# Strassen's form for three pairs of chunks instead of two, x from whole float32 operands, and a planner that counts the port of VectorE and GpSimd

## The chip, the cores and the metric

The kernel runs on one core of a Trainium2 chip. The core has TensorE (PE, matrix products into PSUM), VectorE (DVE), ScalarE (ACT), GpSimd (POOL) and SyncE (SP, which here only issues DMAs). Each engine works through its own list of instructions in order and waits at semaphores. The metric is device time in microseconds (us), lower is better.

## What is computed

```python
kv  = einsum('bhsd,bhse->bhde', k, v)      # 8 batches, 8 heads, s = 576, d = e = 64
o   = einsum('bhsd,bhde->bhse', q, kv)
x   = o / sqrt(mean(o*o, -1) + 1e-6) * g_norm       # per head
x   = x.transpose(0, 2, 1, 3).reshape(4608, 512)    # 4608 tokens, 8 heads x 64
h   = x @ w_in                                      # 512 x 2048
out = (h * cos(h)) @ w_out                          # 2048 x 512
```

All inputs and the output are float32.

## The kernel before

**Tiling.** The 4608 tokens are nine chunks of 512 (`CH`), numbered 0 to 8; the 2048 columns of `h` are 16 blocks `j` of 128 (`NJ`). `NP = 4` is the number of head pairs: the 512 columns of x are four blocks `p` of 128, each of two heads. `x_part(c, p)` makes one such block of one chunk, transposed (128 features by 512 tokens); a chunk covers parts of one or two batches (`chunk_parts`).

**Precision.** The big products are done in a float32 format that TensorE streams at one pass (`F32R`, "fp32r" in the profile). Each operand is split into a high part and a rest (`xhi`, `xlo`; `ghi`, `glo`; two halves of each weight tile), and three products replace one.

**Stage 1 and stage 2, plain.** Step `(c, j)` of `stage1_part` makes block j of h for chunk c: 4 p x 3 products of 512 columns. `act_part` turns it into g = h cos h on ACT and DVE and splits it (`ghi`, `glo`); `stage2_part` multiplies with `w_out`: 4 accumulators (`acc`) x 3 products. Chunks 0 and 1 go first and are interleaved in four segments while the weights are still loaded and split (`w_part`).

**Stage 1 by Strassen's form.** Two chunks and two halves of the 512 features form a 2x2 block product. Seven products of combined operands replace eight. `cross_part` makes the seven combinations of x (adds and splits on POOL or DVE: `adders()` lets the planner choose); `sums_part` makes combined weights on POOL from the split ones, and `keep_in`, `keep_out`, `sums_part` write all weights to DRAM (`wq`, `wod`), since their places in SBUF are then used for the crosses, for x (`raws`) and for g. `quad_part(n)` does the seven products of two blocks j (7 x 6 matmuls) and adds them up through `snap` and `add`; `chain_part` makes g, `split_part` and `gather_part` do stage 2. `load_in` and `load_out` bring the weights back from DRAM for each pair.

Before the change `PLAIN = 5`: chunks 0 to 4 are plain (`NS` = 80 steps), chunks 5, 6 and 7, 8 are two pairs (16 quads).

**x.** For chunks 2 to 8, `kv_part(b)` makes the 64x64 products k'v of one batch in float32: per head pair and head four matmuls of 128 rows and one for the last 64 rows (`k_over`, `v_over`, whose rows 64 to 127 are zero). `kv_parts` writes them to `kv_w` in split form. `x_part` loads q (`q_loads`, eight to sixteen small DMAs), transposes it on DVE (`qT`), splits it for the two heads on ACT and DVE or POOL into tiles `m` and `sg`, multiplies with `kv_w` into two PSUM banks, adds their halves on ACT and DVE, then makes the norm: square (ACT), transpose and sum (DVE), a power -0.5 on POOL (`rinv`), transpose and scaling with `gcol` (DVE). Chunks 0 and 1 use routines of their own (`kv_front_part`, `x_front_part`).

**What sets the order.** The class `Order` is a planner that runs while the program is built: every routine is a generator that asks for time on an engine with a duration, a priority, events and tokens for buffers; the planner always takes the piece that can start first, and that is then the order on the engine (`Pinned`). Priorities come from due times (`due(i)` for step i) plus a table of offsets, `haste`. `gates[i]` fires when step i starts on PE, and routines are let in by it. In the profile every operation has line 206, the helper that records it; operations are told apart by tiles: `bank` are PSUM banks of h, kv, x and transposes, `acc` the accumulators, `wi`/`wo` places of weight tiles, lent to k, v, q at the start and to crosses, g and reloaded weights later.

Of the kernel before, what the change touches and what calls it, by code (L numbers as in the profile page):

```python
# [49 lines left out]
class Order:  # L50
# [11 lines left out]
    def __init__(self):  # L62
        self.busy = {}
        self.pending = []
        self.seq = 0
        self.live = set()
        self.shape = None
# [51 lines left out]
    def ahead(self, e, prio, options):  # L119

        if len(options) == 1:
            return 0.0
        now = self.busy.get(e, 0.0) + 0.2
        return sum(o[0][1] for x, _, t, o, _ in self.pending if len(o) == 1 and o[0][0] == e and x <= prio and t <= now)

    def run(self):
        while self.pending:
            best = None
            for item in self.pending:
                prio, seq, t, options, _ = item  # L130
                ends = [
                    max(t, self.busy.get(o[0], 0.0) + self.ahead(o[0], prio, options)) + o[1] + sum(o[2:])
                    for o in options
                ]
                e, d = options[ends.index(min(ends))][:2]
                start = max(t, self.busy.get(e, 0.0))
                if best is None or (start, prio, seq) < best[0]:
                    best = ((start, prio, seq), item, e, d)
# [8 lines left out]
            end = start + d  # L147
            self.busy[e] = end
# [5 lines left out]
def tile_kernel(  # L154
# [22 lines left out]
    ST = S - SI * P  # L177

# [47 lines left out]
    def dve_only(f):  # L226
        return [("DVE", 0.15 + f / 960)]

    def adders(f=CH, late=0.4):

        return [("POOL", 0.2 + f / 460, 0.0), ("DVE", dve_us(f), late)]
# [7 lines left out]
    kv_w = const.tile([P, 2, H, P], F32R, name="kv_w")  # L239
    warm = const.tile([P, 1], F32, name="warm")  # L240
# [21 lines left out]
    PLAIN = 5  # L262
# [16 lines left out]
    KEEP, SUMS = 34, 40  # L279

    def due(i):
# [7 lines left out]
        ('load q', 0, 1): -62.5, ('acc', 32): 88.0, ('acc', 20): -37.8, ('xd', 7, 3): -3.4, ('unit', 4): 2.6,  # L289
        ('unit', 1): 46.8, ('h', 27): -11.0, ('h', 72): 24.3, ('load q', 1, 1): -3.5, ('cross', 1, 0): 10.5,  # L290
        ('h', 35): 35.9, ('act', 17): 80.9, ('h', 21): -12.0, ('unit', 6): 21.5, ('x', 1, 3): -3.5,
        ('quad', 2): -16.7, ('acc', 21): 19.0, ('load', 'wo', 1): -22.6, ('act', 73): 32.8, ('act', 7): 28.5,
        ('xd', 5, 3): 49.3, ('xd', 6, 1): -11.9, ('acc', 58): 83.2, ('unit', 42): 95.7, ('unit', 11): 45.8,
# [3 lines left out]
        ('h', 70): -15.1, ('act', 0): -23.3, ('load kv', 0, 2): 17.8, ('load', 'wi', 3): 42.2, ('acc', 4): 76.7,  # L297
        ('load kv', 0, 0): 18.4, ('wo', 2): -38.8, ('h', 3): -33.0, ('xd', 8, 0): 70.4, ('load q', 0, 3): 5.7,
        ('h', 58): -11.0, ('acc', 19): -35.6, ('h', 61): -46.5, ('acc', 0): 51.2, ('act', 75): 10.5,
        ('x', 0, 2): 4.0, ('load kv', 0, 3): -7.5, ('h', 75): 26.1, ('acc', 57): 27.1, ('h', 19): 18.3,  # L300
        ('xd', 3, 1): -23.0, ('wo', 12): -1.4, ('h', 12): 8.9, ('xd', 5, 1): -8.5, ('acc', 61): 48.1,
        ('unit', 2): -14.5, ('act', 53): 40.4, ('acc', 9): 10.8, ('h', 68): -6.9, ('acc', 28): 14.4,
        ('h', 42): -9.5, ('h', 65): -5.5, ('act', 65): -18.0, ('h', 60): -4.3, ('wo', 8): 7.8,
        ('split', 13): -14.3, ('quad', 0): -2.5, ('wi', 15): 16.8, ('acc', 18): 12.2, ('xd', 2, 2): -19.3,
    }

    def put_off(*key):
        return haste.get(key, 0.0)

# [57 lines left out]
    def g_part():  # L367
        yield "wait", [g_in]
        yield "run", [("ACT", 0.4)], -11.0
# [14 lines left out]
    def over_loads(b):  # L384
        def issue():
            for t, src in ((k_over, k), (v_over, v)):
                nc.sync.dma_start(out=t[0:ST], in_=src[b, :, SI * P:S, :].rearrange("h p d -> p h d"))
# [116 lines left out]
    def kv_parts(b, srcs, prio):  # L504

        for j, src in enumerate(srcs):
# [9 lines left out]
    def kv_part(b, prio):  # L516
# [36 lines left out]
    def x_front_part(c, p, prio):  # L553
# [53 lines left out]
        yield "run", [("POOL", 1.4)], prio  # L607
# [20 lines left out]
        _, end = yield "run", dve_only(CH), prio  # L628
# [9 lines left out]
    def x_part(c, p, prio):  # L638
# [3 lines left out]
        yield "take", t_two, prio  # L642
# [5 lines left out]
        rows = [slice(j * D, (j + 1) * D) for j in range(2)]  # L648
        qs = [two([P, CH], F32R, j) for j in range(2)]
# [21 lines left out]
        if c < PLAIN:  # L671
            x_slot = yield "take", t_slot, prio
            x = slot_tile(x_slot)
        else:
            held = yield "take", t_raw, prio
            x = store_tile(held)
# [7 lines left out]
        sched.give(t_pair, end)  # L684
# [710 lines left out]
```

## Time and profile before

| | us |
|---|---|
| median of 3 runs | 854.68 (854.52 to 856.24) |
| profiled execution, its own time | 853.01 |
| its span, first to last instruction | 851.2 |
| PE busy / DVE busy / ACT busy / POOL busy | 830.2 / 614.3 / 512.0 / 233.2 |
| chunk 5's first quad starts on PE at about | 500 |

Matmuls are pipelined: the records of 512 columns last 390 ns each and overlap, so a count over a stretch, and not the mean, tells what one costs. A float32 matmul has two records. In a row of a timeline stand the start, the time, the engine, line, operation, tiles, shape and count; in a row by stretches the busy time and the number of instructions of PE, weight loads, DVE, ACT and POOL, then the granted clock, DMA share and GB/s.

### The profile page before, as it was taken

What the parts mean: (1) busy time and instruction counts of PE and PEld (TensorE: products, weight loads), DVE (VectorE), ACT (ScalarE), POOL (GpSimd) and SP (SyncE); (2) the same over time, 40 slices, a digit from 0 to 9 for tenths busy, and PEclk for the clock granted to TensorE, in tenths of its full rate; (3) what the DMA queues carried; (4) which work ended last, traced back from release to release, by engine and by line L of the source; (5) the groups of instructions that cost most, each with busy time, mean ns of one, the idle gap of its engine ahead of it and who ended that gap; (6) DMA issues with size and microseconds to landing.
All of it is one profiled execution on the core that took longest, in us unless ns stands there. A gap on an engine that the chain in (4) does not pass through costs nothing.

```text
span 851.2 us, 12582 instructions
## 1 busy us (share of the span) xinstructions
PE 830.2 (98%) x4400; PEld 686.0 (81%) x4400; DVE 614.3 (72%) x947; ACT 512.0 (60%) x993; POOL 233.2 (27%) x151
## 2 busy tenths in 40 slices
PE   6899999999999999999999999999999999999998
PEld 5778888888888888788888887888788788888886
DVE  2899897489697647868688998899898754445421
ACT  3789685476465547545577657767676554444421
POOL 3220000014135564647313453522444100000000
PEclk9899999999999999999999999999999999999999
DMA  9989746163421324521624357767656566754564
GB/s 304 326 279 380 293 185 223 47 168 96 124 50 51 112 81 129 147 78 54 180 76 113 77 159 219 202 184 217 193 171 237 173 204 194 244 180 143 187 213 144
DMA packets 139968, 145.55 MB, mean 171 GB/s; under 512 B 73216, under 2 KB 112896, under 8 KB 139904
## 3 DMA queue, kind: packets, MB, share of 16 engines
q1 hardware_dynamic: 139392, 144.02, 54.9%
q8 instruction: 35, 0.57, 0.3%
q10 hardware_dynamic: 512, 0.72, 0.2%
q14 instruction: 29, 0.24, 0.1%
HBM read 110.10 MB, written 34.60 MB: 170 GB/s over the span
## 4 chain that ended last, share of the span: by engine, by line
PE 85%; DVE 7%; ACT 2%; issue 2%; POOL 2%; DMA 2%; SPq 1%; ACTq 0%; DVEq 0%; POOLq 0%
PE bank L206 44%; PE acc L206 40%; POOL rinv L206 1%; DVE glo L206 1%; DVE wi L206 1%; DVE wo L206 1%; DVE slot L206 1%; DMA gcol<-in_g_norm_dram 1%; DVE xlo L206 1%; DMA wi<-in_q_dram 1%; DVE qT L206 1%; DVE r L206 1%; ACT wi L206 1%; ACT ki L206 0%; SPq L415 0%
## 5 line engine op out<-in xcount | busy, mean ns | idle before, releaser
L206 PE MATMUL acc<-wo,ghi 128*128 128x512 f32 x1152 | 356.1, 390 | 0.0
L206 PEld LDWEIGHTS acc<-wo,ghi 128*128 128x128 f32 x1152 | 214.8, 188 | 44.1 <-ACT slot L206 0.2
L206 PE MATMUL acc<-wo,glo 128*128 128x512 f32 x576 | 224.5, 390 | 0.0
L206 POOL TENSOR_TENSOR rinv<-ms,mhalf 128x16 f32<-128x16 f32 (+1 forms) x36 | 98.4, 2735 | 306.6 <-DVE ms L206 304.8
L206 PE MATMUL bank<-xhi,wi 128*128 128x512 f32 x576 | 178.3, 391 | 0.0
L206 PE MATMUL bank<-wi,wo 128*128 128x512 f32 (+2 forms) x756 | 165.7, 375 | 4.5 <-DVE wi L206 2.3
L206 PEld LDWEIGHTS bank<-wi,wo 128*128 128x128 f32 (+2 forms) x756 | 128.5, 185 | 34.2 <-DVE wi L206 4.1
L206 PEld LDWEIGHTS acc<-wo,glo 128*128 128x128 f32 x576 | 108.1, 188 | 22.8 <-DVE glo L206 0.2
L206 PEld LDWEIGHTS bank<-xhi,wi 128*128 128x128 f32 x576 | 107.3, 188 | 22.0
L206 PE MATMUL bank<-xlo,wi 128*128 128x512 f32 x288 | 112.2, 390 | 0.0
L206 ACT ACTIVATE ki<-bank 128x512 int32<-128x512 f32 x96 | 57.1, 595 | 55.9 <-PE bank L206 52.8
L206 DVE TENSOR_TENSOR glo<-r,ghi 128x512 fp32r<-128x512 f32 x88 | 66.3, 754 | 23.9 <-ACT ghi L206 22.9
L206 DVE SCALAR_TENSOR_TENSOR r<-bank,ki 128x512 f32<-128x512 f32 x82 | 56.3, 686 | 35.0 <-ACT ki L206 34.0
L206 ACT CAST ghi<-r 128x512 fp32r<-128x512 f32 x89 | 55.2, 620 | 38.9 <-PE acc L206 29.8
L206 ACT ACTIVATE r<-r 128x512 f32<-128x512 f32 x89 | 55.9, 630 | 17.9 <-DVE r L206 17.0
L206 DVE TENSOR_TENSOR r<-r,bank 128x512 f32<-128x512 f32 x82 | 55.7, 681 | 10.9 <-ACT r L206 10.0
L206 PEld LDWEIGHTS bank<-xlo,wi 128*128 128x128 f32 x288 | 54.0, 188 | 11.4
L206 DVE TENSOR_TENSOR glo<-wo,ghi 128x512 fp32r<-128x512 f32 x42 | 31.5, 750 | 36.0 <-ACT ghi L206 34.0
L206 ACT ACTIVATE ki<-wi 128x512 int32<-128x512 f32 x48 | 30.1, 628 | 32.9 <-DVE wi L206 24.9
L206 ACT CAST ghi<-wo 128x512 fp32r<-128x512 f32 x44 | 27.3, 621 | 33.3 <-PE acc L206 31.8
L206 DVE TENSOR_TENSOR wi<-bank,wi 128x512 f32<-128x512 f32 x48 | 32.9, 688 | 11.5 <-PE bank L206 9.4
L206 ACT COPY wi<-bank 128x512 f32<-128x512 f32 x48 | 28.1, 586 | 19.3 <-PE bank L206 18.7
(168 smaller groups left out, 1028.6 us busy)
## 6 DMA issues: line engine op xcount, KB each, us to landing
wo<-wod SPq DMA_DIRECT2D x64, 512.0 KB, 3.4
wo<-wq SPq DMA_DIRECT2D x56, 512.0 KB, 4.2
out_dram<-slot SPq DMA_DIRECT2D x35, 256.0 KB, 2.2
wi<-in_moe_w_in_dram SPq DMA_DIRECT2D x16, 512.0 KB, 8.6
wo<-in_moe_w_out_dram SPq DMA_DIRECT2D x16, 512.0 KB, 8.5
wod<-wo SPq DMA_DIRECT2D x16, 512.0 KB, 5.3
wq<-wi SPq DMA_DIRECT2D x24, 256.0 KB, 4.6
sg<-in_v_dram SPq DMA_DIRECT2D x24, 256.0 KB, 3.9
```

Source lines behind the costliest of these rows:

```text
L206: return lambda *a, **kw: tc.keep_in_program_order(f(*a, **kw))
```

## The change

1. `PLAIN` is 3: chunks 3 and 4 become a third pair, first in time (`NS` = 48 steps, 24 quads). The weights are kept and summed from steps 16 and 18 on instead of 34 and 40, spread over the steps left. A second and third pair's crosses wait for those of the pair ahead.
2. Chunks 2, 3 and 4 (`WHOLE`) get x from `q` and `kv` in whole float32 (`kv_f`): `x_whole` does one matmul per head and part with 64 rows and 64 columns of the array, straight into one bank; the norm (`x_norm`, the old code) reads that bank. The splits and the two banks' additions go.
3. x of chunks 3 and 4 (`ASIDE`) is made in steps 24 to 44, stored to DRAM, and read back when places come free.
4. `k_over`, `v_over` hold a head pair in 128 rows, 64 each, without zeros; their matmuls use 64 rows.
5. The planner: `POOL*` and `DVE*` mark operations with two SBUF operands, and one of them waits for the other (`begin`); durations on POOL are set anew; gates of x and sums can be moved by the table.
6. At the start k and v of the first head pair are issued ahead of all else, and the scaling of `gcol` is planned behind the second pair's loads. The table is new (113 entries for 80).

```diff
     def begin(self, e, t):
+        if e == "POOL*":
+            return max(t, self.busy.get("POOL", 0.0), self.port["DVE"])
+        if e == "DVE*":
+            return max(t, self.busy.get("DVE", 0.0), self.port["POOL"])
+        return max(t, self.busy.get(e, 0.0))
...
-    k_over = const.tile([P, H, D], F32, name="k_over")
-    v_over = const.tile([P, H, D], F32, name="v_over")
-    for t in (k_over, v_over):
-        pool.memset(t[ST:P], 0.0)
+    k_over = const.tile([P, NP, D], F32, name="k_over")
+    v_over = const.tile([P, NP, D], F32, name="v_over")
...
-    PLAIN = 5
+    PLAIN = 3
...
-    KEEP, SUMS = 34, 40
+    KEEP, SUMS = 16, 18
+    WHOLE = (2, 3, 4)
+    ASIDE = (3, 4)
...
     haste = {
-        ('load q', 0, 1): -62.5, ('acc', 32): 88.0, ('acc', 20): -37.8, ('xd', 7, 3): -3.4, ('unit', 4): 2.6,
+        ('kv', 1, 1): 74.8, ('h', 33): 17.7, ('h', 19): 13.3, ('wo', 10): 161.9, ('kv', 0, 3): 15.1,
...
     def g_part():
         yield "wait", [g_in]
+        yield "wait", [kv_in[0, 1]]
...
     def kv_parts(b, srcs, prio):
+        later = [c for c in chunks_of(b) if c >= FRONT]
+        if any(c in WHOLE for c in later):
+            for j, src in enumerate(srcs):
+                _, end = yield "run", [("ACT", act_us(NP * D))], prio
+                act.copy(out=kv_f[j * D:(j + 1) * D, b % 2], in_=src)
+        if all(c in WHOLE for c in later):
+            return end
...
-                        (kt[:, j, i, :], vt[:, j, i, :]) if i < SI else (t[:, 2 * p + j, :] for t in (k_over, v_over)))
+                        (kt[:, j, i, :], vt[:, j, i, :]) if i < SI else (t[r, p, :] for t in (k_over, v_over)))
                     pe.matmul(out=ps[r, p, :], lhsT=lhs, rhs=rhs, start=(i == 0), stop=(i == SI))
...
+    def x_whole(c, p, prio, parts, rows, qT, bank):
+        _, end = yield "run", [("PE", sum(max(0.12, (n + 24) / 600) for _, _, _, n in parts))], -1.0, D
+        ps = ps_tile(bank)[:, 0:CH]
+        for b, s0, o0, n in parts:
+            for r in rows:
+                pe.matmul(
+                    out=ps[r, o0:o0 + n], lhsT=kv_f[r, b % 2, p, :], rhs=qT[r, o0:o0 + n], start=True, stop=True)
+        sched.fire(q_used[c, p], end)
+        sched.give(t_qT, end)
+        x, held = yield from x_place(c, prio)
+        yield from x_norm(c, p, prio, ps, x, held, "DVE", lambda end: give_ps(bank, end))
...
+        if c in ASIDE:
+            _, end = yield "run", [("DMA", 0.9)], prio
+            aside = tc.dram_tile([P, CH], F32, name=f"x{c}_{p}")
+            nc.sync.dma_start(out=aside, in_=x)
+            sched.give(t_slot, end + DMA_LAT, held)
+            stored = Event()
+            sched.fire(stored, end + DMA_LAT)
+            held = yield "take", t_raw, due(begin[PLAIN - 1]) + p
+            yield "wait", [stored]
+            _, end = yield "run", [("DMA", 0.9)], due(begin[PLAIN - 1]) + p
+            x = store_tile(held)
+            nc.sync.dma_start(out=x, in_=aside)
+            end += DMA_LAT
...
-        first, n = (NS + QUAD * NM * (two_chunks - 1), QUAD * NM) if two_chunks else (begin[PLAIN - 1], NJ)
+        first, n = (NS + QUAD * NM * (two_chunks - 1), QUAD * NM) if two_chunks else (begin[PLAIN - 1] - 4, NJ)
...
+        if n:
+            yield "wait", [cross_done[n - 1, q, x] for q in range(7) for x in range(HK)]
...
-            t += put_off("load kv", c, p)
+            t += put_off("load kv", c, p) if c or p else -100.0
...
+            i = min(max(i + step_off("gate x", c, p), last_step[0] + 1 if c < PLAIN else 0), len(gates) - 1)
...
-        sched.spawn(gated(SUMS + 2 * m, sums_part(m, due(SUMS + 3 + 2 * m) + put_off("sums", m))))
+        i = SUMS + m * (NS - SUMS - 6) // NM
+        i = min(max(i + step_off("gate sums", m), 0), len(gates) - 1)
+        sched.spawn(gated(i, sums_part(m, due(i + 3) + put_off("sums", m))))
```

ACT's first instructions before (`wi`/`wo` hold k, v of the first heads, `bank_172` the transposed q):

```order
L206 ACT_TABLE_LOAD
L206 COPY m<-bank_172 128x512
L206 DMA wi_200<-in_k_dram 128x576
L206 DMA wo_201<-in_v_dram 128x576
L206 ACT_TABLE_LOAD
L206 ACTIVATE warm<-warm 128x1
L206 DMA gcol<-in_g_norm_dram 64x1
L206 COPY wo_158<-bank_181 64x64 x2
L206 COPY wo_158<-bank_206 64x64 x2
L206 COPY m<-bank_230 128x512
L206 ACTIVATE gcol<-gcol 64x1 x2
L206 ACTIVATE slot_257<-acc_245 128x512
```

and after:

```order
L222 DMA wi_161<-in_k_dram 128x576
L222 DMA wo_162<-in_v_dram 128x576
L222 ACT_TABLE_LOAD
L222 ACTIVATE warm<-warm 128x1
L222 DMA gcol<-in_g_norm_dram 64x1
L222 COPY wo_157<-bank_173 64x64 x2
L222 COPY m<-bank_198 128x512
L222 ACTIVATE slot_219<-acc_210 128x512
L222 ACTIVATE gcol<-gcol 64x1 x2
```

The loads of k, v and g_norm stand ahead of every computation, one table load is gone, and the first square (`slot`, out of `acc`) stands ahead of the scaling of `gcol`, not behind it.

On PE, the first x part of chunk 2, before:

```order
L206 MATMUL bank_1977<-xlo,wi_1295 128x512
L206 MATMUL bank_1999<-m,kv_w 128x128
L206 MATMUL bank_1999<-m,kv_w 128x384
L206 MATMUL bank_2000<-sg,kv_w 128x128
L206 MATMUL bank_2000<-sg,kv_w 128x384
L206 MATMUL bank_1977<-xhi,wi_1295 128x512 x2
```

and after:

```order
L222 MATMUL acc_1411<-wo_1522,glo 128x512
L222 MATMUL bank_2016<-qT,kv_f 64x128 x2
L222 MATMUL bank_2016<-qT,kv_f 64x384 x2
L222 MATMUL acc_1418<-wo_1522,ghi 128x512 x2
L222 MATMUL acc_1418<-wo_1522,glo 128x512
```

Four matmuls over the whole array into two banks became four over a quarter of it into one, between the same kind of neighbours (stage 1 there, stage 2 here).

On SP, the loads ahead of the first quad's weights, before (chunk 5 is first; `wq` are the weights, `qb` is q of chunks 7 and 8):

```order
L380 DMA m<-in_k_dram 128x2x256
L380 DMA sg<-in_v_dram 128x2x256
L415 DMA qb<-in_q_dram 32x14x32 x4
L415 DMA qb<-in_q_dram 32x2x32 x4
L1064 DMA wo_5254<-wq 128x1024
L415 DMA qb<-in_q_dram 32x14x32 x4
```

and after (chunk 3 is first; `x_3_3475` is the DRAM place of x of chunk 4, pair 3):

```order
L1151 DMA wo_3424<-wq 128x1024
L412 DMA sg<-in_v_dram 128x2x256
L791 DMA x_3_3475<-slot_3292 128x512
L412 DMA sg<-in_v_dram 128x2x256
L799 DMA wo_3044<-x_3_3475 128x512
L1151 DMA wo_3538<-wq 128x1024
L1151 DMA wo_3610<-wq 128x1024
```

A store of x and its reload now stand among the weights' loads, with one other load between them.

More of the change, by code (lines that the diff above doesn't have):

```diff
@@ L63, in __init__ @@
         self.busy = {}
+        self.port = {"POOL": 0.0, "DVE": 0.0}
         self.pending = []
@@ L130, in run @@
                 prio, seq, t, options, _ = item
[L131 to L136, printed above, removed]
+                if len(options) == 1:
+                    e, d = options[0][:2]
+                else:
+                    ends = [
+                        max(t, self.busy.get(o[0].rstrip("*"), 0.0) + self.ahead(o[0].rstrip("*"), prio)) + o[1] + sum(o[2:])
+                        for o in options
+                    ]
+                    e, d = options[ends.index(min(ends))][:2]
+                start = self.begin(e, t)
                 if best is None or (start, prio, seq) < best[0]:
@@ L147, in run @@
             end = start + d
+            if e[-1] == "*":
+                e = e[:-1]
+                self.port[e] = end
             self.busy[e] = end
@@ L226, in dve_only, with pool_us @@
     def dve_only(f):
-        return [("DVE", 0.15 + f / 960)]
+        return [("DVE*", 0.15 + f / 960)]
     def adders(f=CH, late=0.4):
-        return [("POOL", 0.2 + f / 460, 0.0), ("DVE", dve_us(f), late)]
+        return [("POOL*", pool_us(f), 0.0), ("DVE*", dve_us(f), late)]
+    def pool_us(f=CH):
+        return 0.19 + f / 465
     def adder(e):
@@ L239, in tile_kernel @@
     kv_w = const.tile([P, 2, H, P], F32R, name="kv_w")
+    kv_f = const.tile([P, 2, NP, D], F32, name="kv_f")
     warm = const.tile([P, 1], F32, name="warm")
@@ L386, in issue @@
             for t, src in ((k_over, k), (v_over, v)):
-                nc.sync.dma_start(out=t[0:ST], in_=src[b, :, SI * P:S, :].rearrange("h p d -> p h d"))
+                for j in range(2):
+                    nc.sync.dma_start(
+                        out=t[j * ST:(j + 1) * ST],
+                        in_=src[b, :, SI * P:S, :].rearrange("(p two) s d -> two s p d", two=2)[j])
         return issue
@@ L641, in x_part @@
         yield "wait", [q_in[c, p]] + [kv_in[b, n] for b, _, _, _ in parts if b >= FRONT for n in range(NP)]
-        yield "take", t_two, prio
+        if c in WHOLE:
+            yield "wait", [kv_done[b, p] if b >= FRONT else kv_split[b, p] for b, _, _, _ in parts]
+            yield "take", t_psa, prio
+            bank = yield "take", t_bank, prio
+        else:
+            yield "take", t_two, prio
         yield "take", t_qT
@@ L648, in x_part @@
         rows = [slice(j * D, (j + 1) * D) for j in range(2)]
+        if c in WHOLE:
+            yield from x_whole(c, p, prio, parts, rows, qT, bank)
+            return
         qs = [two([P, CH], F32R, j) for j in range(2)]
@@ L728, in x_part @@
         xs[c, p] = xhi, xlo
-        sched.give(t_slot, end, x_slot)
+        sched.give(t_slot, end, held)
         sched.fire(x_done[c, p], end)
@@ L774, in w_part @@
         sched.fire(w_done[key], end)
+    x_reads = {(c, p): sum(1 for x, _, _, _ in steps if x == c) for c in range(PLAIN) for p in range(NP)}
     g_done = [Event() for _ in steps]
```

93 lines of the change are left out of this document (55 added, 38 removed), and 8 rows, old and new, of the table haste.

## The prediction

> **What bounds the kernel now.** I read the page first (busy shares, slices, chain), then stretches of 25 and 75 us, then single rows of the places the change touches.
>
> ```profile
> span 851.2 us, 12582 instructions
> PE 830.2 (98%) x4400; PEld 686.0 (81%) x4400; DVE 614.3 (72%) x947; ACT 512.0 (60%) x993; POOL 233.2 (27%) x151
> PE 85%; DVE 7%; ACT 2%; issue 2%; POOL 2%; DMA 2%; SPq 1%; ACTq 0%; DVEq 0%; POOLq 0%
> ...
> 0.00:25.00 25.00, 16.69 (x232) 15.01 (x233) 7.71 (x18) 10.90 (x27) 7.77 (x15) 0.93 0.98 306
> 25.00:50.00 25.00, 22.34 (x223) 17.86 (x222) 21.87 (x40) 20.16 (x47) 6.55 (x4) 0.93 1.08 346
> 325.00:350.00 25.00, 23.84 (x110) 19.69 (x109) 22.15 (x31) 16.75 (x33) 14.12 (x10) 1.00 0.32 80
> 500.00:525.00 25.00, 22.92 (x166) 17.74 (x165) 23.79 (x30) 18.14 (x35) 15.65 (x9) 1.00 0.63 189
> 525.00:600.00 75.00, 74.50 (x332) 61.51 (x331) 67.48 (x107) 55.46 (x107) 23.47 (x11) 1.00 0.70 199
> 600.00:675.00 75.00, 72.62 (x317) 58.62 (x316) 62.33 (x88) 48.62 (x97) 32.41 (x18) 1.00 0.63 198
> ```
>
> TensorE (PE) is busy 830 of 851 us and is 85% of the chain: the kernel is bound by what PE has to stream, and only three things can move its end: fewer or dearer PE instructions, the 11 us that PE idles in the first 50 us (25 - 16.69 + 25 - 22.34), and the 6.1 us that it idles between 50 and 675 us: 1.16 at 325, 2.08 at 500, where Strassen's form begins, 0.50 and 2.38 while pair 0 runs. In those stretches VectorE (DVE) is at 83 to 95%. What DVE, ScalarE (ACT) or GpSimd (POOL) save elsewhere is hidden.
>
> **The change, part by part.** Terms in us; minus is faster.
>
> *1. Strassen's form for chunks 3 and 4.* Plain, two chunks take 2 x 16 x 12 stage-1 matmuls of 512 columns = 384; a pair takes 8 x 7 x 6 = 336. Stage 2 has 192 per chunk in both forms. So 48 fewer.
>
> ```profile
> 105.19 2.72 PE acc L206 x12
> ```
>
> Twelve such matmuls in a row take 2.72, so 0.227 each: 48 x 0.227 = -10.9, all of it on the path. The pair's work on the other engines comes with it: 24 more copies and adds and the seven operands' splits, counted under 6.
>
> *2. x of chunks 2 to 4 from whole float32 operands.* Twelve parts (3 chunks x 4 head pairs). The old part on PE, and what float32 in half tiles costs:
>
> ```profile
> 177.80 0.40 PE L206 MATMUL bank<-xlo,wi 128*128 128x512 f32 x1
> 178.04 0.45 PE L206 MATMUL bank<-m,kv_w 128*128 128x128 f32 x2
> 178.62 0.62 PE L206 MATMUL bank<-xhi,wi 128*128 128x512 f32 x2
> ...
> 14.23 1.26 PE L206 MATMUL bank<-wi,wo 64*64 64x64 f32 x36
> 15.43 0.66 PE L206 MATMUL bank<-ident,wi 128*128 128x128 f32 x4
> ...
> 224.46 0.39 PE L206 MATMUL bank<-xlo,wi 128*128 128x512 f32 x1
> 224.78 0.69 PE L206 MATMUL bank<-sg,m 128*64 128x64 f32 x16
> 225.41 0.64 PE L206 MATMUL bank<-sg,m 128*64 128x64 f32 x16
> 225.99 0.64 PE L206 MATMUL bank<-sg,m 128*64 128x64 f32 x16
> 227.26 0.73 PE L206 MATMUL bank<-xhi,wi 128*128 128x512 f32 x2
> 227.82 0.40 PE L206 MATMUL bank<-xlo,wi 128*128 128x512 f32 x1
> ```
>
> The old part runs from 178.04 to 178.62: 0.59 with its late start. A float32 matmul has two records, so the kv rows show five pairs of 64-column matmuls in 225.99 - 225.41 = 0.58, 0.116 for a pair of heads. The row at 14.23 shows the new part's own tile, 64x64 with both heads at once: nine pairs in 1.20 with its ends, the same pace. 512 columns are eight such pairs, 0.93 (a long matmul has fewer starts, so this is the upper end of the pace). Then the change of tile: the kv block starts 0.09 late (224.46 + 0.23 against 224.78), its first group takes 0.63 instead of 0.58, its four groups and their end take 0.16 more than 4 x 0.58, and the third matmul behind comes after 0.56 instead of 0.46. That is 0.35 for going in and out, of which 0.14 (0.09 + 0.05) is going in. New part: 0.93 + 0.35 = 1.28, 0.69 more than 0.59, x 12 = +8.3. From below: the same without any cost of the change of tile, 0.34 x 12 = +4.1. From above: the two heads one after the other, 2 x 0.93 + 0.35 = 2.21, +19; the row at 14.23 speaks against that. I take +8.3. ACT and DVE lose two copies, two subtractions, two copies and two adds per part; they pay where DVE is full (6).
>
> *3. The last 64 rows of k and v in 64-row tiles.* Two head pairs now share one 128-row tile, so two of the ten matmuls of each head pair use 64 rows of the array, while the other eight still use 128. Their number and pace stay, but a kv block now changes tile seven more times inside, six batches: 42 changes. No row of before changes rows alone. Bounds: nothing, 0, and the dearer direction above, 0.35 - 0.14 = 0.21 each, +8.8. Nearest is the change into a narrow tile, whose refill is a 64-column one here too: 42 x 0.14 = +5.9. The Trainium skill, TensorEngine Tiling (Array Packing), section Key Properties, says that changing the tiling mode, and not just the tile, drains the engine, and lists 128x64 and 64x64 as different modes; by it the +5.9 stands, and by a rule that only columns matter it would be 0. Rows of before cannot decide that.
>
> *4. The start.* ACT's first instruction was a copy that waited for PE; behind it stood k and v of the first heads and the load of g_norm.
>
> ```profile
> 0.72 1.28 ACT L206 ACT_TABLE_LOAD   x1 [0.72 <-PEq L1379]
> 5.52 0.58 ACT L206 COPY m<-bank 128x512 f32<-128x512 f32 x1 [3.51 <-PE bank L206]
> 7.12 0.39 ACTq L206 DMA_DIRECT2D wi<-in_k_dram  x1
> 8.85 1.28 ACT L206 ACT_TABLE_LOAD   x1 [2.75 <-DMA wi<-in_q_dram]
> 9.95 5.93 DMA gcol<-in_g_norm_dram
> 15.90 0.43 ACT L206 ACTIVATE gcol<-gcol 64x1 f32<-64x1 f32 x2 [3.84 <-DMA gcol<-in_g_norm_dram]
> 10.58 0.87 ACT L206 COPY wo<-bank 64x64 f32<-64x64 f32 x4 [0.24 <-issue]
> 11.50 2.37 PE L206 MATMUL acc<-wo,m 128*128 128x128 f32 x16 [1.68 <-ACT wo L206]
> 16.24 1.05 ACT L206 ACTIVATE slot<-acc 128x512 f32<-128x512 f32 x2
> 16.85 0.69 DVE L206 TENSOR_REDUCE ms<-slot 128x8 f32<-128x512 f32 x1 [4.87 <-ACT slot L206]
> 20.36 0.63 PE L206 MATMUL acc<-ident,r 128*128 128x128 f32 x4 [4.27 <-DVE r L206]
> wi<-in_k_dram ACTq DMA_DIRECT2D x1, 288.0 KB, 6.7
> 35.08 0.71 PE L206 MATMUL bank<-xhi,wi 128*128 128x512 f32 x2
> ```
>
> Now the two loads are ACT's first rows, one table load is gone, and the square that feeds the first reduction stands ahead of gcol. k issued at 0.75 lands at 7.45 by its own 6.7; kv takes 1.2 (the 64x64 row above), copies 0.9, x0 on PE 1.2 (half of 2.37), the square 0.5 (half of 1.05): the first reduction at 11.3 instead of 16.85, -5.5. PE idles 4.27 behind that reduction and loses clock after it (0.93 over 25 us), so the room is there. Bounds: 0 if the 300 GB/s of the first stretch set the start anyway, and -13 if all idle time there went. I take -5.5.
>
> *5. Parking chunks 3 and 4.* Eight stores and eight loads of 256 KB on SP's queue.
>
> ```profile
> part<-slot SPq DMA_DIRECT2D x8, 256.0 KB, 4.2
> slot<-part SPq DMA_DIRECT2D x8, 256.0 KB, 2.6
> ```
>
> 4.2 + 2.6 = 6.8 from x to x again; while a reload waits for its store, the weights' loads behind it on SP wait too. For seven parts the steps of chunk 2 cover it. The last, x of chunk 4's fourth pair, is loaded two rows behind its store, between the first and the second load of the quads' weights; the planner allows 2.9 for each way, so it comes 1.0 later than planned: +1.0 at the first quad, between 0 and 6.8. Keeping the split weights in DRAM some hundred us earlier meets DMA engines that are a third busy (0.32 at 325 us): hidden.
>
> *6. Two stretches instead of one.* Chunks 5, 6 get their x during pair 0 and 7, 8 during pair 1, by the old route: the idle time of 525 to 675 us (2.88) can come twice, +2.9. Against it: chunks 2 to 4 load DVE less (1.16 at 325), and DVE and POOL stand in each other's way today:
>
> ```profile
> 264.66 0.67 DVE L206 TENSOR_TENSOR glo<-r,ghi 128x512 fp32r<-128x512 f32 x1
> 267.02 1.51 POOL L206 TENSOR_TENSOR sg<-sg,slot 128x512 f32<-128x512 f32 x1 [2.92 <-ACT slot L206]
> 267.30 1.79 DVE L206 TENSOR_TENSOR glo<-r,ghi 128x512 fp32r<-128x512 f32 x1
> ```
>
> The same subtraction takes 1.79 while POOL works and 0.67 alone; the new order counts that and gives POOL 36 of the splits instead of 13, some 23 x 0.67 = 15 us off DVE in these stretches. I put relief (-3.9: 2.88 and 1.0) against both, so 5 and 6 together 0, between -4 and +8.
>
> **Sum:** -10.9 + 8.3 + 5.9 - 5.5 + 0 = -2.2. The profiled execution took 853.01 (span 851.2); that gives 850.8. The median of the runs shown is 854.68, 1.7 higher, and the same difference from it gives **852.5**. 0.2% is 1.7 us, about what a measurement of this kernel tells from no change.
>
> **Rivals.** *Changes of rows cost nothing* (3 is 0): -8.1, 846.6. For it: no row of before shows such a cost. Against: every change of tile that is shown does cost.
>
> *The parked x is late (slower side).* Place: the first quad, whose second product needs all four parts of chunk 4. Price: the whole 6.8 of store and reload instead of the 1.0 in part 5, so 5.8 more, 858.3. It decides from 3.9 on (2.2 + 1.7). For: store and reload stand next to each other on SP, and PE idles 2.08 at that place already. Against: five steps of stage 2 (60 matmuls, 13.6 us) now stand between chunk 2's last stage-1 matmul and the first quad, where before three stood.
>
> *POOL's port (slower side).* The sums over the weights, POOL operations of up to 1.5, move beside the twelve x parts, 24 steps of 5.44 (two rows of 2.72) or five windows of 25. If each of the 28 subtractions there were held by the 1.12 that the two rows differ, DVE would lose 31 us and be as full throughout as it is at 325 us: 5 x 1.16 less the 1.16 that is there already, +4.6, 857.1. It decides from 3.9 on. Against: the new order counts the port, and x parts out of PSUM leave DVE fewer operations there. The Trainium skill, SBUF — State Buffer, section SBUF: two separate sides, calls the shared port an exclusive lock for the whole instruction; the pair of rows at 267 agrees; that the lock is whole and not partial no row shows.
>
> *The start is set by the loads* (4 is 0): +3.3, 858.0. For: the DMA engines are full in both first stretches.
>
> **Chances.** My forecast 0.48 (within some 3 us: faster 0.6, same 0.3, slower 0.1), free changes of rows 0.17, parked x 0.13, port 0.12, start 0.10. Faster 0.29 + 0.17 + a tenth of the rest 0.04 = 0.50; same 0.14 + a quarter of the rest 0.09 = 0.23; slower 0.27. The range reaches from below the free-rows case to past the parked x, 844 to 860; the likeliest case alone has 849 to 856.
>
> **What will show it.** PE matmuls 4400 records less 48 on 512 columns; x rows (out of qT and kv_f) near 1.28 a part; the kv block some 1 us longer than 2.67 from 224.69 to 227.36; the first reduction near 11 us and the first stage-1 matmul well ahead of 35.08; the idle time at the first quad 3 us at most; PE idle in both stretches near 3 us. It is wrong if a kv block keeps its length, if x parts cost double, or if PE idles over 10 us between 50 us and the end.

## The result and the profile after

| | us |
|---|---|
| kernel before, median of 4 runs | 854.6 (852.43 to 856.24) |
| changed kernel, median of 4 runs | 846.8 (845.88 to 847.48) |
| ratio, with its 95% interval | 0.991 (0.9885 to 0.9934) |
| span of the profiled execution, before and after | 851.2 and 844.6 |

The change made the kernel 7.8 us faster; forecast were 2.2. The page of the changed kernel:

```profile
span 844.6 us, 12739 instructions
PE 830.7 (98%) x4400; PEld 677.0 (80%) x4400; DVE 592.7 (70%) x903; ACT 497.7 (59%) x971; POOL 272.0 (32%) x176
```

PE is busy as long as before (830.2): the time gained is idle time of PE, and the work that the change adds on PE is made up for by the fuller clock at the start (ahead of the landmark below PE is busy 156.4 us instead of 158.8). The same stretches as before, and 225 to 250, which is new:

```profile
0.00:25.00 25.00, 20.85 (x302) 18.38 (x302) 12.84 (x28) 15.04 (x38) 10.46 (x15) 1.00 0.97 314
25.00:50.00 25.00, 23.74 (x218) 18.38 (x217) 21.84 (x40) 20.94 (x46) 6.44 (x3) 1.00 1.08 347
225.00:250.00 25.00, 22.30 (x158) 16.95 (x157) 15.78 (x24) 9.44 (x23) 12.66 (x9) 0.93 0.54 155
325.00:350.00 25.00, 24.66 (x175) 19.92 (x174) 17.70 (x24) 17.57 (x34) 14.83 (x12) 1.00 0.83 242
500.00:525.00 25.00, 25.00 (x113) 20.68 (x112) 23.07 (x34) 19.48 (x35) 5.90 (x4) 1.00 0.75 196
525.00:600.00 75.00, 75.00 (x333) 61.99 (x332) 57.30 (x88) 48.13 (x97) 27.27 (x14) 1.00 0.69 210
600.00:675.00 75.00, 74.45 (x329) 61.34 (x328) 56.31 (x74) 45.98 (x83) 24.24 (x15) 1.00 0.66 207
```

The first 50 us lose 5.4 us of PE idle (50 - 20.85 - 23.74) instead of 11.0, and at full clock instead of 0.93. The idle time at 325, 500, 525 and 600, 6.1 us before, is 0.9; in its place there are 2.7 us in 225 to 250, again with a clock of 0.93.

One landmark splits the time. Ahead of the first kv block of chunk 2 both kernels have the same 1011 matmul records on PE. Its first row in the timeline of PE, before:

```profile
169.72 0.69 PE L206 MATMUL bank<-sg,m 128*64 128x64 f32 x16
```

And after, with the block to its end and the first x part behind it:

```profile
162.22 0.69 PE L222 MATMUL bank<-sg,m 128*64 128x64 f32 x16
162.84 0.33 PE L222 MATMUL bank<-v_over,k_over 64*64 64x64 f32 x4
163.10 0.69 PE L222 MATMUL bank<-sg,m 128*64 128x64 f32 x16
...
165.73 0.73 PE L222 MATMUL acc<-wo,ghi 128*128 128x512 f32 x2
...
168.69 1.08 PE L222 MATMUL bank<-qT,kv_f 64*64 64x128 f32 x8
169.71 0.73 PE L222 MATMUL acc<-wo,ghi 128*128 128x512 f32 x2
```

So of the span's -6.6 us, -7.5 come from the start (169.72 to 162.22), and all the rest of the program together costs +0.9. In the rest, a head pair's period in the kv block is 163.10 - 162.22 = 0.88 instead of 0.58, and an x part takes 1.02 from its first matmul to the next wide one.

The start itself, in the timeline of ACT, DVE and PE:

```profile
10.00 0.60 ACT L222 ACTIVATE slot<-acc 128x512 f32<-128x512 f32 x1 [1.25 <-PE acc L222]
10.63 0.69 DVE L222 TENSOR_REDUCE ms<-slot 128x8 f32<-128x512 f32 x1 [2.13 <-ACT slot L222]
23.76 0.71 PE L222 MATMUL bank<-xhi,wi 128*128 128x512 f32 x2
```

The first reduction is at 10.63 (16.85 before, 11.3 forecast), the first stage-1 matmul at 23.76 (35.08 before).

And the new idle time, in the timelines of SP, ACT, DVE and PE:

```profile
224.16 4.00 SPq L450 DMA_DIRECT2D qb<-in_q_dram  x8
228.25 0.40 SPq L791 DMA_DIRECT2D x<-slot  x1
228.75 0.88 SPq L1107 DMA_DIRECT2D wq<-sg  x2
229.73 0.41 SPq L799 DMA_DIRECT2D xhi<-x  x1
...
232.66 0.62 ACT L222 CAST wi<-xhi 128x512 fp32r<-128x512 f32 x1 [3.08 <-DMA xhi<-x]
...
233.31 1.59 DVE L222 TENSOR_TENSOR wi<-xhi,wi 128x512 fp32r<-128x512 f32 x1 [3.01 <-ACT wi L222]
...
238.33 0.68 DVE L222 STREAM_TRANSPOSE qT<-qb 128x512 f32<-128x512 f32 x1
...
239.07 1.75 PE L222 MATMUL bank<-qT,kv_f 64*64 64x192 f32 x8 [2.70 <-DVE qT L222]
```

SP issues one DMA after another, 0.4 to 0.5 us each; the reload of parked x (`xhi<-x`, L799) stands behind eight loads of q, a store of x and two of weights. ACT's split copy for the first cross waits 3.08 for it, DVE's subtraction waits 3.01 for that copy, and behind five more DVE rows comes the transposition of q on which PE waits 2.70. The reload is not all of it: POOL works on `sg<-wi` from 233.06 on and on `m<-sg,m` from 234.43 on (1.29 and 1.63), and beside it DVE's two subtractions for the cross take 1.59 and 1.18 instead of 0.67, together 1.4 of the 2.70. The x part behind the wait then takes 1.68 (240.75, the next wide matmul, less 239.07) instead of 1.02: half clock.

### The profile page after: what moved, and what is told of

Read it like the earlier page. It is cut to its first block, busy times and chain, and to the rows that moved or that the text cites. A ratio compares the mean times of both kernels' runs of the same rounds, so it can differ in the third digit from the quotient of the medians.

```text
span 844.6 us, 12739 instructions
## 1 busy us (share of the span) xinstructions
PE 830.7 (98%) x4400; PEld 677.0 (80%) x4400; DVE 592.7 (70%) x903; ACT 497.7 (59%) x971; POOL 272.0 (32%) x176
## 4 chain that ended last, share of the span: by engine, by line
PE 83%; DMA 5%; DVE 4%; SPq 2%; POOL 2%; ACT 2%; issue 1%; DVEq 0%; POOLq 0%; ACTq 0%
PE acc L222 42%; PE bank L222 41%; SPq L450 1%; DMA wo<-in_moe_w_out_dram 1%; POOL rinv L222 1%; DMA wi<-in_moe_w_in_dram 1%; DMA wi<-in_q_dram 1%; DVE r L222 1%; DMA wo<-in_v_dram 1%; DVE wi L222 1%; DVE glo L222 0%; DMA qb<-in_q_dram 0%; DVE wo L222 0%; DMA wi<-in_k_dram 0%; SPq L1107 0%
## 5 line engine op out<-in xcount | busy, mean ns | idle before, releaser
L222 PE MATMUL bank<-wi,wo 128*128 128x512 f32 (+2 forms) x1092 | 243.5, 377 | 0.3 <-DVE xlo L222 0.3
L222 PEld LDWEIGHTS bank<-wi,wo 128*128 128x128 f32 (+2 forms) x1092 | 191.4, 184 | 40.7 <-DVE xlo L222 0.8
L222 PE MATMUL bank<-xhi,wi 128*128 128x512 f32 x320 | 100.2, 394 | 0.5 <-DVE xlo L222 0.5
L222 PEld LDWEIGHTS bank<-xhi,wi 128*128 128x128 f32 x320 | 59.0, 188 | 15.8 <-issue 3.0
L222 DVE TENSOR_TENSOR glo<-r,ghi 128x512 fp32r<-128x512 f32 x59 | 44.0, 747 | 34.9 <-ACT ghi L222 34.5
L222 PE MATMUL bank<-xlo,wi 128*128 128x512 f32 x160 | 62.3, 389 | 0.0
L222 ACT CAST ghi<-r 128x512 fp32r<-128x512 f32 x59 | 36.5, 619 | 35.3 <-PE acc L222 29.4
L222 ACT ACTIVATE wo<-wo 128x512 f32<-128x512 f32 x69 | 43.3, 628 | 17.6 <-DVE wo L222 17.2
L222 DVE SCALAR_TENSOR_TENSOR wo<-wi,ki 128x512 f32<-128x512 f32 x52 | 40.0, 770 | 9.1 <-ACT ki L222 8.8
L222 DVE SCALAR_TENSOR_TENSOR r<-bank,ki 128x512 f32<-128x512 f32 x51 | 35.0, 685 | 15.1 <-ACT ki L222 14.5
```

Of the source, the lines that this page charges most:

```text
L222: return lambda *a, **kw: tc.keep_in_program_order(f(*a, **kw))
```

## Experiments

### The 64-row tiles alone, in the kernel before

```diff
-    k_over = const.tile([P, H, D], F32, name="k_over")
+    k_over = const.tile([P, NP, D], F32, name="k_over")
...
-    (t[:, 2 * p + j, :] for t in (k_over, v_over))
+    (t[r, p, :] for t in (k_over, v_over))
```

(As in the change, the rows are also loaded by two DMAs instead of one, and the two fills with zeros at the start go.)

> The kernel before with one part of the change alone: the last 64 rows of k and v of two heads share one 128-row tile and are multiplied in 64-row tiles. Order, counts and sizes of all else are those of before. If a change of rows of the array costs what a change of columns costs, each of the six kv blocks changes tile seven more times inside: its length goes from 2.69 to about 3.72 us (7 x 0.147), and the time rises by 6.2 us (+0.7%), from about 854.6 to about 860.8. Rival: only a change of columns has a price; blocks stay at 2.69 and the time stays within 1 us. Second rival: the kv blocks lie on the path only in part, since PE idles elsewhere; blocks of 3.72 but a rise of less than 4 us.

Measured: 858.64 against 854.37, ratio 1.0048 (1.0032 to 1.0064), that is +4.3 us. One of its blocks:

```profile
226.52 0.69 PE L206 MATMUL bank<-sg,m 128*64 128x64 f32 x16
227.13 0.33 PE L206 MATMUL bank<-v_over,k_over 64*64 64x64 f32 x4
...
230.02 0.73 PE L206 MATMUL bank<-xhi,wi 128*128 128x512 f32 x2
```

From its first matmul to the next wide one the block takes 3.50, where before it took 2.48 (224.78 to 227.26 in the prediction's rows): +1.02, or 0.146 for each of seven changes. So a change of rows costs about what the change of columns into a narrow tile did (0.14). All six blocks take 21.0 us instead of 15.1 in the profiled executions, +5.9. The total rises by less, as the second rival had it in part: PE's waits at 500 us became 1.0 us shorter.

### The kv block grouped by tile

```diff
-        for p in range(NP):
-            for i in range(SI + 1):
+        for i0, i1 in ((0, SI), (SI, SI + 1)):
+            for p, (kt, vt) in enumerate(srcs):
+                for i in range(i0, i1):
```

In this first form every head pair begins its sum anew in the shared bank while others are open, so part of kv's products is lost; number and kind of the instructions are those of the changed kernel.

> The changed kernel, with the matmuls of a kv block in another order: those of 128 rows of all four head pairs first, then those of 64 rows of all four. Same matmuls, same tiles, same order of all else. Theory (each change of tile costs about 0.147 us): one change inside a block instead of seven, 36 fewer in six blocks; a block goes from 3.72 to about 2.83 us, the time falls by 5.3 us (-0.6%). Rival: 64-row matmuls are slow themselves (weights loaded into half of the rows, or a write to PSUM that waits), so that a block stays near 3.7 and the time does not move.

Measured: 843.22, ratio to the kernel before 0.9864 (0.9843 to 0.9885).

```profile
202.65 2.09 PE L222 MATMUL bank<-sg,m 128*64 128x64 f32 x64
204.66 0.68 PE L222 MATMUL bank<-v_over,k_over 64*64 64x64 f32 x16
205.28 0.73 PE L222 MATMUL bank<-xhi,wi 128*128 128x512 f32 x2
...
228.69 0.41 SPq L802 DMA_DIRECT2D xhi<-x  x1
...
238.15 1.97 PE L222 MATMUL bank<-qT,kv_f 64*64 64x192 f32 x8 [3.49 <-DVE qT L222]
```

The block takes 2.63 (205.28 - 202.65): 0.88 less than 3.51 with six changes less, 0.147 each, and 0.15 more than the 2.48 without any. The rival of slow 64-row matmuls falls. Of the 5.3 us some 3.6 arrive: PE came to the wait near 236 us 1.7 us earlier, and the wait's end moved by only 0.9 (239.07 to 238.15), so that the wait grew from 2.70 to 3.49; and the half clock there lasted 6.8 us instead of 3.4 (granted clock 0.86 over 225 to 250 us instead of 0.93).

The Trainium skill, TensorEngine Tiling (Array Packing), section Key Properties, says that a change of mode drains the engine; the runs agree: 0.147 us between 128x64 and 64x64 in float32.

### ACT's start alone, in the kernel before

```diff
+            issue = kv_loads_front(c, p, lend(2, [kv_used[c, p]]))
+            if not (c or p):
+                issue()
+                issue = lambda: None
```

(The planner still sees the load at its old place, so that nothing else moves.)

> The kernel before with the start of the change alone: ACT issues k and v of the first heads and the load of g_norm ahead of its first copy; nothing else moves. My prediction put -5.5 us on it. Theory now: it is worth more, because the two idle stretches of PE at the start also led to half clock: first reduction near 10.7 us instead of 16.85, PE idle in the first 50 us from 11.0 to about 5.5, granted clock from 0.93 to 1.00 in both first stretches of 25 us, and the time falls by 8 to 10 us. Rival 1: the clock does not change with it, -5.5. Rival 2: the earlier start in the changed kernel came from the other moves of the table (x parts and loads in another order), and alone this is worth 0 to -2.

Measured: 849.87 against 854.37, ratio 0.9948 (0.9927 to 0.9969): -4.5 us. Its timeline on DVE and PE:

```profile
13.91 0.69 DVE L206 TENSOR_REDUCE ms<-slot 128x8 f32<-128x512 f32 x1 [1.66 <-ACT slot L206]
...
165.40 0.69 PE L206 MATMUL bank<-sg,m 128*64 128x64 f32 x16
```

and by stretches:

```profile
0.00:25.00 25.00, 19.54 (x272) 17.50 (x272) 10.87 (x25) 13.63 (x34) 8.98 (x16) 0.93 0.96 316
25.00:50.00 25.00, 23.77 (x227) 18.82 (x228) 22.68 (x41) 20.70 (x47) 5.54 (x5) 0.93 1.08 342
```

The landmark moves by 4.3 us (169.72 to 165.40), and the clock stays at 0.93 in both stretches. This is rival 1 within the interval: alone, the early loads are worth what they save in idle time. The theory of 8 to 10 fell for this edit; the clock had to come from elsewhere.

### Idle PE time filled with zeros, in the kernel before

```diff
+        if c == 0 and p in (1, 0):
+            idle = ps_o.tile([P, DM], F32, name=f"acc{0 if p else 3}")
+            for _ in range(56 if p else 24):
+                pe.matmul(out=idle[:, 0:P], lhsT=zeros, rhs=zeros, start=True, stop=True)
         for a in range(NTT):
             pe.transpose(...)
```

> The kernel before with 56 and 24 matmuls of zeros (128 columns, bfloat16, into an accumulator that nobody reads) put into two idle stretches of PE at the start, the 4.27 us ahead of the row at 20.36 and the 1.78 us ahead of that at 30.70. They take some 3.1 and 1.3 us, less than the idle time, so nothing waits for them. Theory (idle time of PE lowers its clock for 3.4 us afterwards, at half speed, 1.7 us lost each): granted clock 1.00 instead of 0.93 in both first stretches of 25 us, the time falls by 3.4 us, and the scatter between 851 and 856 us becomes smaller. Rival: the clock follows something else (power, the float32 matmuls), and nothing changes: 0.

Measured: 850.31 against 854.73, ratio 0.9954 (0.9941 to 0.9966): -4.4 us, and its five runs lie between 849.53 and 851.04, where the kernel before has 852.45 to 855.31. One row of PE, and the stretches:

```profile
11.74 3.89 PE L206 MATMUL acc<-wo,m 128*128 128x128 f32 x16 [1.68 <-ACT wo L206]
...
0.00:25.00 25.00, 21.34 (x296) 19.67 (x297) 7.43 (x18) 11.05 (x27) 7.77 (x15) 0.93 0.97 303
25.00:50.00 25.00, 23.68 (x272) 18.76 (x274) 23.85 (x44) 22.11 (x51) 6.55 (x4) 1.00 1.08 349
```

Work that nobody needs made the kernel faster, so the clock follows PE's idle time. In the profiled execution one spell is left in the first stretch, now near 12 us, behind a wait of 1.68 that was not filled. The kernel before has the same wait in front of the same 16 matmuls, and they took 2.37 there (the prediction's row at 11.50): the same wait is followed by half clock in one execution and not in the other.

### Both together: the start of the changed kernel, rebuilt

> The kernel before with ACT's new start (k, v and g_norm issued first) and matmuls of zeros in the three idle stretches of PE that the run with that start alone showed (26 ahead of the first kv product, 14 and 24 ahead of two transpositions of x). Theory: the start of the changed kernel is these two things and nothing else, an earlier first product and no half clock: the first kv block of chunk 2 begins near 162 us as in the changed kernel (169.7 before, 165.4 with ACT's start alone), granted clock 1.00 in both first stretches, and the time falls by 7 to 8 us. Rival: the two gains are the same idle time counted twice, so that both together give no more than one of them, 4 to 5 us; then the other 3 us of the changed kernel's start come from its table.

Measured: 847.22 against 855.38, ratio 0.991 (0.9891 to 0.993): -8.2 us.

```profile
0.00:25.00 25.00, 21.90 (x333) 20.16 (x334) 11.76 (x26) 14.52 (x37) 9.88 (x17) 1.00 0.97 306
25.00:50.00 25.00, 24.93 (x244) 19.60 (x241) 23.85 (x44) 21.95 (x47) 6.98 (x5) 1.00 1.08 341
```

```profile
163.06 0.69 PE L206 MATMUL bank<-sg,m 128*64 128x64 f32 x16
```

The landmark is at 163.06, 6.7 before the old place and 0.8 behind the changed kernel's; the clock is 1.00. The gains add up, and the rival falls. An earlier first product and a full clock at the start give as much as the whole change: the kernel before with these two edits and without any Strassen pair more runs in 847.2, the changed kernel in 846.8.

### The wait near 236 us: the reload planned later

```diff
-            end += DMA_LAT
+            end += DMA_LAT + (2.0 if c == 3 else 0.0)
```

> The changed kernel, where the planner counts 2.0 us more for the way back of chunk 3's parked x. The only moves are near 230 us: the third block's difference goes from GpSimd to VectorE, and the two split copies of the first crosses on ACT and their subtractions stand two to three rows further back. Theory (ACT and VectorE stood behind a reload that had not landed): the idle time of 2.70 us on PE near 236 us goes below 1 us, the half-clock spell of 3.4 us behind it goes too (granted clock 1.00 there instead of 0.58), the time falls by 3 to 4 us. Rival A: the transposition of q was late by itself, VectorE being full there: the idle time stays near 2.7 and the time too. Rival B: the idle time goes but the slow clock stays, because it has another cause: -2.7 only.

Measured: 845.89, ratio to the kernel before 0.9902 (0.9885 to 0.992); its interval covers the changed kernel's 0.991.

```profile
230.84 0.41 SPq L799 DMA_DIRECT2D xhi<-x  x1
...
234.42 0.69 DVE L222 TENSOR_TENSOR wi<-xhi,wi 128x512 fp32r<-128x512 f32 x1 [2.67 <-ACT wi L222]
...
239.28 1.08 PE L222 MATMUL bank<-qT,kv_f 64*64 64x192 f32 x8 [1.46 <-DVE qT L222]
```

The idle time went from 2.70 to 1.46 and the slow clock with it, but I read this wrongly at first as the edit's doing (the shift of 2.9 and 2.8 in later expectations). PE comes back at 239.28, not earlier than in the changed kernel (239.07); it only got there 1.5 us later, because this execution had a longer start (the landmark is at 163.70). The end of the wait hangs on SP's reload: 229.73 and 239.07 in the changed kernel, 228.69 and 238.15 with grouped blocks, 9.3 and 9.5 us apart. Here it is 230.84 and 239.28, 8.4 apart: DVE's subtraction began 0.03 us ahead of POOL's addition and took 0.69 instead of 1.59. In a later kernel with the same edit (the grouped block with the reload planned later) it took 1.64 again, so this too is no effect of the edit.

### The crosses held back

```diff
-        yield "wait", [x_done[a11]]
+        yield "wait", [x_done[a11]] + ([] if n else [gates[36]])
```

with the grouped block, where now only the first matmul into each half of the bank begins a sum (`start=(p == 0 and i == 0)`).

> The changed kernel with two edits. First, the kv block in grouped order as in the run before, where now only the first matmul into each half of the bank begins a sum anew, so that kv is whole. Second, the first pair's crosses wait until step 36 has begun on PE; by that the two split copies on ACT and their subtractions that stood behind the reload of parked x near 230 us come some seven rows later. What follows in the plan moves too. Theory: blocks of 2.83 instead of 3.72 us (-5.3), the idle time of 2.70 us near 236 us and the half-clock spell behind it gone (-2.9 at that place, measured as the shift between the two kernels' matmuls across it, as the run with the reload planned later gave it), together about -8 against the changed kernel's 846.8: 838 to 840. Rival: the crosses come too late for the first quad, or the wait appears at another x part, and only the -5.3 remains: 841 to 843.

Measured: 848.95, ratio 0.9936 (0.9922 to 0.995): slower than with the grouped block alone, and outside both the theory and the rival. The wait near 236 us is gone, as the x part there shows, and others stand in its place (waits of PE in the whole program: total, times, longest):

```profile
233.99 1.08 PE L222 MATMUL bank<-qT,kv_f 64*64 64x192 f32 x8
```

```profile
PE bank L222 <- DMA wo<-wq: 3.5, 1, 3.5
PE acc L222 <- ACT slot L222: 2.4, 1, 2.4
```

So the split copies of reloaded x did stand in the way of q's transposition; but later crosses moved the rest of the plan, and its new waits cost more than the 2.7 us.

### One chunk back to the old x route, and a planner without the port

```diff
-    WHOLE = (2, 3, 4)
+    WHOLE = (2, 3)
```

> The changed kernel with chunk 4's x by the old route (q split for two heads, two banks added), chunks 2 and 3 still from whole float32. The plan is made anew with the same table. On PE four parts cost 0.545 instead of 1.22 us: -2.7. Theory: x from whole float32 is a bad bargain only where VectorE has room; in steps 30 to 44 it has (18.3 of 25 us busy in 200 to 225), so that most of the -2.7 shows: -1 to -3. Rival: the additional copies, subtractions and adds of four parts, some 4 x 5 us on ACT and VectorE, make q's transposition or the crosses late; PE idles more than 2.7 us longer, and the time rises.

Measured: 861.27, ratio to the kernel before 1.0085 (1.0069 to 1.0101).

```profile
PE bank L222 <- DMA wo<-wq: 6.7, 1, 6.7
```

```diff
-        if e == "POOL*": ...
+        return max(t, self.busy.get(e.rstrip("*"), 0.0))
```

> The changed kernel with a planner that does not count the shared port (an operation of GpSimd or VectorE with two operands in SBUF begins without regard to the other's). The plan is made anew with the same table; VectorE gets some 27 operations more, GpSimd fewer. Theory (the prediction's relief of 3.9 us in its sixth step): without the count the additions on GpSimd and VectorE collide again, PE idle behind 50 us rises by about 4 us, and so does the time. Rival: the count moves operations but saves PE nothing, since VectorE is not on the path in most places: within 1.5 us of the changed kernel.

Measured: 858.77, ratio to the kernel before 1.005 (1.0035 to 1.0065).

```profile
PE acc L218 <- DVE glo L218: 4.9, 1, 4.9
```

Both are 12 to 14 us slower than the changed kernel. The first went the way of its rival and the second the way of its theory (+4), but by far more than either had a reason for. Between 225 and 400 us, where crosses, parked x and the weights' stores meet, PE idles 15.1 us in the first and 11.7 in the second, against 3.0 in the changed kernel, with half clock behind the longest waits. They tell little on what they were meant for: each makes the plan anew with a table of offsets that was found for another plan, as the gated crosses did. What whole float32 operands and the port count are worth apart from the table stays open.

### The grouped kv block and the later reload together

The grouped block (whole kv) with the reload planned later:

> The changed kernel with the kv blocks grouped (only the first matmul into each half of the bank begins a sum anew) and the way back of chunk 3's parked x planned 2.0 us longer: the two edits that moved few instructions. Theory: blocks of 2.83 us (36 fewer changes of tile, -5.3), and the shift across the place near 236 us as in the run with that edit alone (-2.8); no new wait of more than 1 us behind it. 846.8 - 8 gives about 839, ratio to the kernel before about 0.982. Rival: the two gains overlap or a later wait takes them back as in the run with gated crosses: 843 or more.

Measured: 842.13 (841.63 to 844.72), ratio to the kernel before 0.9862 (0.9835 to 0.9889): some 4.7 us less than the changed kernel. The rival held: PE reached the x part earlier and waited 3.46 for it (the first subtraction of the cross again took 1.64).

```profile
228.34 0.41 SPq L802 DMA_DIRECT2D xhi<-x  x1
...
237.65 1.76 PE L222 MATMUL bank<-qT,kv_f 64*64 64x192 f32 x8 [3.46 <-DVE qT L222]
```

### Fewer DMAs ahead of the reload on SP

```diff
-                    nc.sync.dma_start(out=wq[:, 7 * m + q, n], in_=...)
+                    (nc.sync if n else act).dma_start(out=wq[:, 7 * m + q, n], in_=...)
```

> The changed kernel with grouped kv blocks, and the stores of the weight sums' high parts (32 DMAs of the whole program) issued by ACT, which makes them, instead of SP. PE, VectorE and GpSimd keep their order. In four kernels so far PE came back at the x part near 236 us 8.4 to 9.5 us after SP had issued the reload of parked x (229.73 and 239.07 in the changed kernel, 228.69 and 238.15 with grouped blocks), whenever PE itself was ready; and SP issues without a pause from 216 us on, 0.4 to 0.5 us for each DMA. Theory (SP's issue time sets the stall): four of these stores, 1.9 us, leave SP's queue ahead of the reload, it is issued near 226.8 and PE comes back near 236.3: idle time from 3.5 to about 1.6 us, 842 to 843 us become about 840. Rival: the reload waits for its store or for VectorE and is issued at 228.7 as before: no change, or worse by ACT's 0.4 us for each issue.

Measured: 841.74 (839.4 to 842.81), ratio 0.9854 (0.9827 to 0.988).

```profile
226.92 0.48 SPq L802 DMA_DIRECT2D xhi<-x  x1
...
230.33 0.62 ACT L222 CAST wi<-xhi 128x512 fp32r<-128x512 f32 x1 [2.82 <-DMA xhi<-x]
...
236.77 1.08 PE L222 MATMUL bank<-qT,kv_f 64*64 64x192 f32 x8 [2.41 <-DVE qT L222]
```

The reload is issued 1.8 us earlier than with grouped blocks alone, as forecast, and PE comes back 1.4 us earlier; it waits 2.41, not 1.6, as the reload took 0.5 longer to its reader and PE came there 0.3 earlier.

With the low parts on GpSimd's queue too (`nc.sync` becomes `pool`):

> As the other kernel of this call, and the stores of the sums' low parts issued by GpSimd, which makes them: SP has none of these 64 stores left, eight of them (3.7 us) ahead of the reload. Theory: the reload is issued near 225 us, PE comes back at once (it is ready at 234.7), idle time there below 0.5 us, no half clock behind it: 837 to 839 us, ratio to the kernel before about 0.98. Rival: GpSimd needs so long for an issue that its sums and the powers for the norm come late, and PE waits for these: 842 or more.

Measured: 841.54 (840.58 to 843.52), ratio 0.9856 (0.9834 to 0.9878).

```profile
222.92 3.84 SPq L450 DMA_DIRECT2D qb<-in_q_dram  x8
...
227.37 0.38 SPq L802 DMA_DIRECT2D xhi<-x  x1
```

The theory reached only as far as SP was busy: it is now free ahead of 222.92, but the loads of q wait for their buffer, and the reload still stands behind them, at 227.37 instead of 225, and takes 4.6 to its reader on ACT instead of 2.9. The forecast of 837 to 839 was missed, and so was that of about 840 for the edit before. The four kernels with grouped blocks and without held-back crosses cannot be told apart by their times (841.5 to 843.2); all are faster than the changed kernel and the kernel before.

## Why the prediction was right, and where not

The direction and the range held; the amount was too small, 2.2 for 7.8 us.

1. **48 fewer wide matmuls, -10.9.** The count is right: 2757 wide records behind the landmark for 2805 (the x parts have 48 more, so the total stays 4400). The price was tested by no run by itself; the sum of the program behind the landmark agrees with it (below).
2. **x from whole float32, +8.3.** Right, with some luck. A part takes 1.01 to 1.02 from its first matmul, and 1.21 with the late start and the slow first wide matmul behind it (forecast 1.28). The old parts of chunks 2 to 4 took 0.58, 0.52 and 0.49, 0.53 on average (the prediction took the dearest, 0.59, for all), so +0.68 x 12 = +8.2: both numbers were too big by about the same.
3. **64-row tiles, +5.9.** Right, and shown twice: +1.02 a block alone in the kernel before, -0.88 a block when six of seven changes go. The six blocks of the changed kernel take 21.0 us for 15.1, +5.9. The rival with free changes of rows falls. The price was taken from the change into a narrow tile, the nearest row, and that was the right neighbour.
4. **The start, -5.5.** This term was mis-sized: -7.5 in the two profiled executions. Its mechanism is right and its first reduction too (10.63 for 11.3). What it left unpriced is the clock, which the prediction named in half a sentence (0.93 over 25 us). In the profiled execution of before, two spells of half clock, 3.4 us long each, cost 1.7 each; filling PE's idle time alone brought 4.4, the early loads alone 4.5, both 8.2. The rival that the loads set the start falls. The medians differ by 1.2 us more than the two profiled executions: that of before has a granted clock of 0.995, and half of its runs have 0.992 or less (last section).
5. and 6. **Parking and two stretches, 0 between -4 and +8.** Behind the landmark the program takes 0.9 longer; terms 1 to 3 give -10.9 + 8.2 + 5.9 = +3.2, so 2.3 are left as a gain, inside the bounds. The parts came out otherwise than I put them. No wait at the first quad, and no idle time repeated in the second stretch: the waits of 6.1 us shrank to 0.9 in those stretches. In their place stands the parked x, not at the first quad (328.7 us), as the rival had it, but 90 us earlier, where the first cross already wants it: 2.7 us, and slow clock behind it (0.66 in the x part alone, 1.68 for 1.02). Most of the 2.3 can be found in the starts of the matmuls around the waits, since a wait costs more than the idle time that the profile shows. Behind the landmark the waits lengthen the way from one matmul to the next by 8.5 us in all before (6.1 idle) and by 5.0 after (4.1 idle), and the half clock near 240 us by 1.6: 1.9 less together. The last 0.4 stay open.

The rival of POOL's port fell as to its place (PE idles 0.3 at 325). That collisions go on is seen in the stall: the DVE row of 1.59 at 233.31 is the same subtraction that takes 0.67 alone, and with the 1.18 of the second one they are, by these rows, about half of the new wait.

The Trainium skill, TensorE: Matmul & The Clock Gate, section Part 1: The HAM clock gate, says that the clock halves after an idle window of about 3.4 us. The spells' length agrees. The wait's does not: 2.70 us were enough in the changed kernel, and in the kernel before 1.78 us, 0.66 us of work behind a wait of 0.88. So a wait is to be priced with the clock behind it, and not at its own length alone.

## What to carry to other kernels

Price an idle stretch of PE with the clock that follows: here a wait of some 2 us could cost 1.7 us more, and 80 matmuls of zeros in the first 30 us brought 4 us. Count changes of tile, not matmuls, where small products of different row counts alternate, and order the loops by tile shape. A wait whose end is set by another queue (here SP's, 0.4 to 0.5 us for each DMA, and VectorE beside GpSimd) gets longer when the engine that waits arrives earlier: look at what time it ends in several kernels before you say what ended it.

## What the runs showed of the hardware

- A change between 128x64 and 64x64 float32 tiles costs 0.147 us, the mean of both directions: 2.48, 2.63 and 3.51 us for the same 80 records with none, one and seven changes.
- Waits of PE of 1.4 to 5.0 us were followed by half clock in some executions, for 3.4 us or, behind some of the longer waits (3.49 with grouped blocks, 4.95 with the 64-row tiles alone), for 6.8. The same wait can be followed by none: 1.68 near 11.5 us (none in the kernel before, a spell with the zeros), 1.41 near 510 us (none in the kernel before, clock 0.93 over 500 to 525 us with ACT's start alone).
- This goes with most of the scatter of the kernel before: of its 18 runs beside the first experiments, the nine of 850.9 to 854.0 us have a granted clock of 0.994 to 0.996 and the nine of 854.8 to 856.0 us one of 0.989 to 0.992. With the idle time filled, the runs lie between 849.5 and 851.0 at 0.996 to 0.999.
- A VectorE subtraction of 128x512 with two operands in SBUF takes 0.67 to 0.69 alone and 1.34 to 1.79 when a GpSimd addition has begun ahead of it (five kernels near 232 us, and the prediction's pair at 267).
- A sum that is begun anew in a PSUM bank spoils the open sums in other columns of the same bank and partitions, which is why the grouped block begins only one in each half of the bank. The Trainium skill, PSUM — Partial Sum Buffer, section The four PSUM rules, states this, and the grouped kernels agree: with a beginning for each head pair the output is off by a relative error of 1.10, with one for each half of the bank the sums are whole.
